# Two loads of first-layer weights begun later, one turn of R moved, and an earlier order put back, in a fused RWKV-7 and mixture kernel

## The chip, the cores and the metric

The kernel runs on one core of one Trainium2 chip. The metric is the device time of one execution in microseconds (us); the time before is the median of three runs. Profiles are of one execution each, with times counted from the start of its span.

## What is computed

The reference has two blocks. The first is an RWKV-7 recurrence over 768 tokens for 4 batches of 8 heads with 40 columns each. The second takes its output as 3072 rows of 320 columns and runs four two-layer experts (320 to 1024 to 320), mixed by given probabilities. All is in fp32.

```python
for t in range(S):                       # S = 768, state is D x D per head, D = 40
    y[:, :, t] = einsum('bhd,bhde->bhe', rt, state)
    Sa = einsum('bhde,bhe->bhd', state, at)
    state = state * wt[:, :, None, :] - einsum('bhd,bhe->bhde', Sa, bt)
    state = state + einsum('bhd,bhe->bhde', vt, kt)
...
p = domain_probs / (domain_probs.sum(-1, keepdims=True) + 1e-09)
for e in range(E):                       # E = 4
    h = np.maximum(x @ w1[e], 0.0)
    out += p[:, e:e + 1] * (h @ w2[e])
```

## The kernel before, in words

The recurrence is computed in chunks of 64 tokens. A *unit* is one chunk of two batches, so there are 24 units, numbered from 0. The work of a unit is split into generators, each advanced step by step with `run(generator, n)`, and the order of these calls is the order of TensorE's program:

- `within(q)` does what needs no state: it turns R and V (`turn_rv`), scans the decays (G), turns the tokens (NT, KT), and makes the scores (pc, pfe with pe, pev). In unit 1 its second step turns V and its third turns R: four transposes into `pRT` on TensorE and three copies into `RT` on ScalarE.
- `substitute(q)` solves a triangular system in blocks of 32: `M` is made by VectorE, and Z is built by VectorE in the first two units and by GpSimd in all later ones.
- `merge(q)` turns the solution (Qc, QTc) and makes two products, `pY` and `pQ`. Each is taken out of PSUM by four copies on ScalarE.
- `step(q)` joins unit and state: psat and pst, then `pxr`, then `pdy`, then xT, which the mixture takes as input.

The mixture runs on TensorE between these steps. w1 is loaded in *pieces* (half an expert: one DMA of 512 KB and two of 64 KB, `load_piece`); piece k serves the k-th product `ph`. A product has two parts: `up_last`, small matmuls for the last 64 input columns, and `up_main`, the large ones (8 and 8 in the program, 16 and 16 in the profile, which shows an fp32 matmul twice); the function `lead()` does `up_last` alone, ahead of its turn. w2 is loaded an expert at a time (`load_w2`, 1280 KB). From unit 2 on the second layer is done for two units at once by seven products (`p431`, `p75`, `p26`), whose PSUM tiles share three buffers with the two tiles of each `ph`. VectorE adds them to the output by `add`, and these additions are named out0, out1 and so on; out12 and out13 are the two that read the first `p75` of the first pair of units.

Three things set the order. TensorE goes in program order. VectorE's order is written by hand in `VECTOR_ORDER` (lines 20 to 30): each name is made to stand behind the one ahead of it. SyncE's queue gets the loads in the order of the calls, and each load takes one of eight DMA semaphores in turn, so that a load waits until the eighth load ahead of it has landed. The natural (not turned) B and K of a unit, `natB` and `natK`, have one buffer each: the loads for unit 2 wait until unit 1's n_tok and k_tok are made.

The start of unit 1 and the first pieces stand in the code so:

```python
load_piece()
load_piece()
run(m)
run(ws[1], 2)
go(load_raw(units[2], "A"))
load_w2(0)
load_piece()
load_piece()
run(ws[1], 1)
```

Here `m` is `merge(units[0])`, which has just made `pY`, and `ws[1]` is `within(units[1])`. Later comes `load(units[2], "BK")`, then `load_w2(1)`. In the loop over units, `EARLY` is 5; in iteration 5 a `lead()` stands between a step of `within` and the step of `step` that makes `pxr`.

Of the kernel before, what the change touches and what calls it, by code (L numbers as in the profile page):

```python
# [23 lines left out]
    YG3 SG3.0 S+3.1 gp5 SG3.1 1/gp5 RT5 N5 K5 sum_w4 out7 VC5.1 VC5.0 Qc4 QTc4 ET5.0 blocks5.0 blocks5.1 ET5.1 M5  # L24
    M05 Z15 Z25 RH4.0 RH4.1 G6.0 G6.1 gl6 G06 scan6 sum_a4 gll6 sum_w5 sum_w6 AT6 AG6 sum_a0 sum_a1 sum_a2 sum_a3
    SX4.0 SX4.1 sum_w7 VT6 sum_w8 Y4.1 Y4.0 S+4.0 YG4 SG4.0 S+4.1 gp6 SG4.1 1/gp6 RT6 N6 K6 out8 out9 out10 out11
    sum_a5 VC6.1 VC6.0 Qc5 QTc5 out12 out13 ET6.0 blocks6.0 blocks6.1 ET6.1 M6 M06 Z16 Z26 out14 out15 sum_w9 sum_a6
    G7.0 G7.1 gl7 G07 RH5.0 RH5.1 scan7 gll7 sum_a7 sum_a8 sum_a9 AT7 AG7 out16 out17 out18 out19 sum_w10 sum_w11
    SX5.0 SX5.1 sum_w12 sum_w13 sum_w14 sum_a10 sum_a11 out20 sum_a12 out21 sum_a13 VT7 out22 sum_a14 out23
"""  # L30
# [3 lines left out]
def kernel(  # L34
# [38 lines left out]
    nc = tc.nc  # L73
# [14 lines left out]
    names, made, stated_order = VECTOR_ORDER.split(), {}, []  # L88
# [273 lines left out]
    def load_w2(e):  # L362
        tc.keep_in_program_order(nc.sync.dma_start(out=w2_sb[e][:], in_=moe_w2[e].rearrange("(f p) d -> p f d", p=P)))
# [19 lines left out]
    def quarter(q):  # L383
        return slice(Q * q, Q * q + Q)

    def of_slot(x, s):

        return x.rearrange("p (j s) e -> p j s e", s=2)[:, :, s, :]
# [59 lines left out]
    def within(q):  # L448
# [19 lines left out]
        def turn_rv(which="VR"):  # L468
            VT = None
            if "V" in which:  # L470
                VT = sb.tile([P, 2 * NJ, L], FP32, name="VT", tag="turned", bufs=3)
            if "R" in which:
                q.RT = sb.tile([P, 2 * NJ, L], FP32, name="RT", tag="RT", bufs=2)
            for x, t in (("V", VT), ("R", getattr(q, "RT", None))):
                if x not in which:
                    continue
                if q.u >= PADDED:
                    noted(turn_raw(t[:], n["raw" + x][:]), x + "T", q.u)
                    continue
                p = turn(f"p{x}T", tok(n["padded" + x]), q.u == 1)[:].rearrange("p (j i t) -> p j i t", i=2, t=L)  # L480
                to = t[:].rearrange("p (i j) t -> p j i t", i=2)
                places = [(to[:, 0::2], p[:, 0::2])]
                places += [(to[half(r), 1::2], p[half(1 - r), 1::2]) for r in range(2)]
                for at, (o, p_) in enumerate(places):
                    if q.u == 2 and (x == "R" or at == 2):
                        noted(nc.vector.tensor_copy(out=o, in_=p_), x + "Tc", q.u, at)
                    else:
                        nc.scalar.copy(out=o, in_=p_)
            return VT

        if q.u == 1:
# [172 lines left out]
    def merge(q):  # L664


        Qc = sb.tile([P, H, Q], FP32, name="Qc", tag="q", bufs=2)
        QTc = sb.tile([P, H, Q], FP32, name="QTc", tag="q", bufs=2)
        keep(noted(nc.vector.transpose(out=dealt(Qc[:]), in_=q.Z), "Qc", q.u))
        ins = nc.vector.transpose(  # L670
            out=QTc[:].rearrange("p h r -> p (h r)"), in_=Qc[:].rearrange("p h c -> p (h c)"),
        )
        keep(noted(ins, "QTc", q.u))
        q.QT = QTs()
        for i in range(P // Q):
            ins = nc.gpsimd.tensor_copy(out=q.QT[quarter(i), :, quarter(i % 2)], in_=QTc[quarter(i)])  # L676
            tc.keep_in_program_order(ins)
        yield

        def two_heads(name, lhsT, rhs, to):  # L680
            p = big(name)
            for n in range(NJ):
                for r in range(2):
                    matmul(
                        out=p[half(r), n * 2 * Q:(n + 1) * 2 * Q], lhsT=lhsT[half(r), 2 * n:2 * n + 2, :],
                        rhs=rhs[half(r), 2 * n:2 * n + 2, :], start=True, stop=True,
                    )
            for r in range(2):
                for y in range(2):
                    src = p[quarter(2 * r + y), 0:H * Q].rearrange("p (n two t) -> p n two t", two=2, t=Q)[:, :, y, :]  # L690
                    with sooner(name == "pY"):
                        nc.scalar.copy(out=of_slot(to[quarter(2 * r)], y), in_=src)

        Y = Ys()
        two_heads("pY", q.below, QTc, Y)
        yield

        two_heads("pQ", Qc, Y, q.QT[:, :, quarter(1)])
        yield

# [357 lines left out]
    def run(gen, n=99):  # L1058
        if gen is None:
            return  # L1060
        for _ in range(n):
            if next(gen, gen) is gen:
                break
# [53 lines left out]
        load_padded(units[2], x)  # L1117
    load_piece()
    load_piece()
    run(m)  # L1120
    run(ws[1], 2)
    go(load_raw(units[2], "A"))
    load_w2(0)
    load_piece()
    load_piece()
    run(ws[1], 1)
    run(s, 3)
    run(ws[1], 1)
# [1 line left out]
    run(ws[1], 1)  # L1130
    run(s)
    load(units[2], "BK")
    load_w2(1)
    load_piece()
    run(ws[1], 2)
# [39 lines left out]
    for u in range(1, NU):  # L1175
        in_order[0] = True
        q = units[u]
        m = s_next = w = w_next = iter(())
        if u + 1 < NU:
            m, s_next = merge(units[u + 1]), begin_step(u + 1)  # L1180
            w_next = ws[u + 1]
        if u + 2 < NU:
            w = ws[u + 2]

        def gap(n, pieces=None):
            here[0] = at = 4 * u + n
            run(sum_ops, sums_at.get(at, 0))
            mix((1 if at in sparse else 2) if pieces is None else pieces)

        early = u < EARLY  # L1190
        if early:
            begin_later(len(later))
        ahead = u + 3 < NU and u in range(EARLY, EARLY + 3)
        if ahead:
            go(load_raw(begin(u + 3), "W"))
        if early:
            lead()
        if u == 1:
            run(s, 1)
            run(w_next)  # L1200
        else:
            run(w_next, 99 if early else 1)
            if u == EARLY:
                lead()
            run(s, 1)
        gap(0)


        if early:
            run(s, 1)  # L1210
        run(w, 1)
        if not early:
            run(w_next)
            run(s)

        if early:
            run(w, 1)
            gap(1, 2 if u + 1 == EARLY else None)
            run(s)
        if u == 1:  # L1220
            mixture_of_unit(q)
        elif q.bp:
            mixture_of_chunk(units[u - 1:u + 1], chunks_x[q.c])
        if not early:
            begin_later(len(later))
            run(w, 1)
            lead()
            todo[:2] = todo[1::-1]
            gap(1)
            run(m, 1)  # L1230

        if u + 3 < NU:
            if u == 1:
                go_now(load_raw(begin(4), "WVRA"))
            else:
                go(load_raw(units[u + 3] if ahead else begin(u + 3), "A" if ahead else "WA"))
            load(units[u + 3], "WBKV")
            if u > 1:
                later.extend(load_raw(units[u + 3], "VR"))
        run(w, 2)  # L1240

        soon = u in (2, 3, 4)
        if soon:
            run(w, 1)
        if early:
            run(m, 1)
        else:
            run(m, 1)
            run(s_next, 1)
            lead()  # L1250
            run(m, 1)
            if u + 3 < NU:
                ws.append(within(units[u + 3]))
                run(ws[u + 3], 1)
        if soon:
            substitute(units[u + 2], nc.gpsimd)
        gap(2)

        if u == 1:
            run(s_next, 1)  # L1260
            run(m, 1)
        if not soon:
            run(w, 1)
        if not soon and u + 2 < NU:
            with sooner(not early):
                substitute(units[u + 2], nc.gpsimd)
        if not early:
            lead()
            run(s_next, 1)
        if early:  # L1270
            run(w, 1)
        if early:
            ws.append(within(units[u + 3]))
            run(ws[u + 3], 1)
            if u > 1:
                run(m, 1)
                run(s_next, 1)
            run(m)
            if u == 3:
                begin_later(len(later))  # L1280
            gap(3, 1)
            run(s_next, 1)
        else:
            begin_later(len(later))
            gap(3)
        s = s_next
# [1 line left out]
    for piece in last:  # L1288
        piece()
    moved = [(out_, x) for out_, a_, u_ in ((45, 27, 9), (61, 37, 10)) for x in (f"sum_a{a_}", f"AT{u_}")]  # L1290
    for one, then in [*zip(names, names[1:]), *((f"out{n}", x) for n, x in moved), ("blocks0.3", "VCv1")]:
        tc.add_manual_dep(made[then].ins, made[one].ins.name, BEHIND, reason="stated order of VectorE")
    for k, then in ((13, "SX2.1"), (22, "SX5.0")):
        tc.add_manual_dep(made[f"piece{k}"].ins, made[then].ins.name, AFTER, reason="weights not beside dense products")
# [28 lines left out]
```

## Time and profile before

| What | Value |
|---|---|
| Median of three runs | 1083.35 us (1083.32 to 1083.89) |
| The profiled execution's own time | 1083.35 us |
| Its span in the profile | 1081.6 us, so 1.75 us lie around it |
| Mean granted TensorE clock | 0.996 |
| TensorE matmul busy | 1063.6 us (98%) |
| VectorE, GpSimd, ScalarE busy | 762.6, 492.7, 352.8 us |
| DMA | 122.19 MB, mean 113 GB/s |
| Chain that ended last | TensorE 92%, VectorE 3%, ScalarE 2%, DMA 1%, SyncE's queue 1%, issue 1% |

A span is read from its stages: the shares of the whole span hide the first 50 us, in which TensorE is not dense, and short stretches in which another engine is the one that never rests. "Issue" as the end of a wait means that the profile shows nothing that the engine waited for.

### The profile page before, as it was taken

The page shows a single profiled execution, that of the slowest core. Times are in us where ns is not written, and L with a number is a line of the kernel's source. Part 1 is how long each engine was busy: PE and PEld are TensorE (multiplying, and loading weights), DVE is VectorE, ACT ScalarE, POOL GpSimd, SP SyncE. Part 2 cuts the span into 40 slices and gives each one's busy share as a digit, 9 for nine tenths or more (in the row PEclk, how much of TensorE's full clock was granted, in tenths as well). Part 3 has the DMA queues.
Part 4 walks back from the last instruction along what each step waited for, and adds up shares of the span by engine and source line. Part 5 has one row for each costly group of instructions (what it writes and reads, how often), then busy time and mean ns, then how long its engine had stood idle before and what let it go on. Part 6 is the DMA issues. An engine that isn't in the chain of part 4 may idle for free.

```text
span 1081.6 us, 38611 instructions
## 1 busy us (share of the span) xinstructions
PE 1063.6 (98%) x16140; PEld 957.3 (89%) x16140; DVE 762.6 (71%) x1553; ACT 352.8 (33%) x954; POOL 492.7 (46%) x1274
## 2 busy tenths in 40 slices
PE   7899999999999999999999999999999999999998
PEld 7788888889999999999999999999999999998887
DVE  8777679897777866877777768668767776634343
ACT  3442434333333423324333334233233333221110
POOL 5216777755264373373562653733735626520000
PEclk9999999999999999999999999999999999999999
DMA  6877654445436445444354364454444532322320
GB/s 114 247 213 171 145 115 121 81 109 141 99 86 156 99 112 128 110 114 116 95 130 101 94 148 94 103 129 111 108 95 113 127 88 61 99 86 69 104 74 13
DMA packets 268869, 122.19 MB, mean 113 GB/s; under 512 B 213736, under 2 KB 242072, under 8 KB 268696
## 3 DMA queue, kind: packets, MB, share of 16 engines
q1 hardware_dynamic: 264872, 119.02, 45.5%
q8 instruction: 127, 2.08, 0.8%
q10 hardware_dynamic: 3824, 0.71, 0.4%
q14 instruction: 46, 0.38, 0.1%
HBM read 111.79 MB, written 3.93 MB: 107 GB/s over the span
## 4 chain that ended last, share of the span: by engine, by line
PE 92%; DVE 3%; ACT 2%; DMA 1%; SPq 1%; issue 1%; ACTq 0%; DVEq 0%
PE ph L110 39%; PE p L110 30%; PE po L110 3%; PE pdy L110 3%; PE pxr L110 2%; PE psat L110 2%; PE prn L110 2%; PE pfe L110 1%; PE pc L110 1%; PE pev L110 1%; PE pQ L110 1%; PE pe L110 1%; PE pNT L113 1%; PE pg L113 1%; PE pY L110 1%; PE pKT L113 1%
## 5 line engine op out<-in xcount | busy, mean ns | idle before, releaser
L110 PE MATMUL ph<-xT,w1p 128*128 128x256 f32 (+3 forms) x3040 | 441.3, 375 | 0.4 <-issue 0.4
L110 PEld LDWEIGHTS ph<-xT,w1p 64*64 64x64 f32 (+1 forms) x3040 | 336.5, 161 | 54.0 <-issue 13.8
L658 POOL TENSOR_TENSOR Z<-Z 128x31 f32<-128x31 f32 (+7 forms) x704 | 261.8, 372 | 55.2
L969 DVE TENSOR_TENSOR a<-hs 128x512 f32<-128x512 f32 x220 | 153.6, 716 | 106.2 <-ACT hs L846 106.2
L846 ACT ACTIVATE hs<-ph 128x512 f32<-128x512 f32 (+1 forms) x208 | 117.1, 564 | 321.5 <-PE ph L110 320.8
L645 POOL TENSOR_TENSOR Z<-M,Z 128x62 f32<-128x62 f32 (+7 forms) x352 | 144.4, 410 | 95.1 <-DVE M L631 69.2
L110 PE MATMUL p<-sums,a 128*128 128x160 f32 x1056 | 164.9, 299 | 0.0
L861 DVE SCALAR_TENSOR_TENSOR osb<-p,gate,osb 128x320 f32<-128x320 f32 (+1 forms) x243 | 107.9, 481 | 66.7 <-PE p L110 61.6
L110 PEld LDWEIGHTS p<-sums,a 128*128 128x128 f32 x1056 | 152.8, 190 | 2.2
L612 POOL COPY below<-F 32x256 f32<-32x256 f32 x48 | 21.3, 443 | 230.1 <-ACT F L567 228.5
L110 PEld LDWEIGHTS p<-w,hs 128*128 128x128 f32 x704 | 98.6, 190 | 8.9 <-issue 7.7
L110 PE MATMUL p<-w,hs 128*128 128x160 f32 x704 | 104.9, 302 | 0.3 <-DVE osb L861 0.3
L110 PE MATMUL p<-w,a 128*128 128x160 f32 x704 | 102.8, 299 | 0.0
L110 PEld LDWEIGHTS p<-w,a 128*128 128x128 f32 x704 | 98.0, 190 | 0.0
L676 POOL COPY QT<-QTc 32x256 f32<-32x256 f32 x96 | 40.4, 421 | 75.3 <-DVE QTc L670 67.1
L766 ACT COPY RS<-pxr 64x256 f32<-64x256 f32 x88 | 32.3, 367 | 104.4 <-DVE SX L446 51.6
L596 ACT COPY EV<-pev 64x160 f32<-64x160 f32 x96 | 23.0, 286 | 92.6 <-PE pev L110 92.3
L511 DVE RECIPROCAL gp<-gp 128x320 f32<-128x320 f32 x24 | 51.6, 2151 | 0.7
L615 DVE STREAM_TRANSPOSE M<-blocks 128x1024 f32<-128x1024 f32 x24 | 47.3, 1969 | 2.9 <-ACT blocks L608 2.9
L446 DVE COPY_PREDICATED VC<-mask_up,pc 128x256 f32<-128x256 int32 x48 | 18.7, 444 | 39.2 <-PE pc L110 39.2
L567 ACT COPY F<-pfe 128x256 f32<-128x256 f32 x48 | 15.6, 376 | 82.4 <-PE pfe L110 80.2
L110 PE MATMUL pdy<-VC,k_tok 64*64 64x104 f32 (+1 forms) x768 | 38.2, 259 | 0.0
(150 smaller groups left out, 1341.5 us busy)
## 6 DMA issues: line engine op xcount, KB each, us to landing
w1p<-in_moe_w_dram SPq DMA_DIRECT2D x95, 512.0 KB
w1p<-in_moe_w_dram SPq DMA_DIRECT2D x190, 64.0 KB
w<-in_moe_w_dram SPq DMA_DIRECT2D x4, 1280.0 KB
sums<-in_moe_w_dram SPq DMA_DIRECT2D x9, 512.0 KB
natW<-in_w_dram SPq DMA_DIRECT2D x48, 80.0 KB
natB<-in_b_dram SPq DMA_DIRECT2D x48, 80.0 KB
natK<-in_k_dram SPq DMA_DIRECT2D x48, 80.0 KB
out_dram<-osb SPq DMA_DIRECT2D x46, 80.0 KB
```

Source lines behind the costliest of these rows:

```text
L110: return stated(nc.tensor.matmul(**k))
L113: return stated(nc.tensor.transpose(**k))
L511: pin(noted(nc.vector.reciprocal(out=gp[:], in_=gp[:]), "1/gp", q.u))
L596: nc.scalar.copy(out=of_slot(q.EV[half(p)], i ^ p)[:, :, 0:D], in_=pev[i][half(p)])
L615: ins = nc.vector.transpose(out=M[:], in_=cols)
L645: ins = eng.tensor_tensor(out=Z[:, 1:3, 0:n, j + 1:Q], in0=M[:, j:j + 2, None, j + 1:Q].to_broadcast([P, 2, n, m]), in1=Z[:, here, 0:n, j: ...
L658: eng.tensor_tensor(out=z[:, 0], in0=z[:, 0], in1=z[:, x], op=ALU.add)
L676: ins = nc.gpsimd.tensor_copy(out=q.QT[quarter(i), :, quarter(i % 2)], in_=QTc[quarter(i)])
L766: nc.scalar.copy(out=RS[half(s), x ^ s::2], in_=prs[x][half(s)].rearrange("p (j i) t -> p j i t", i=2),)
L846: ins = nc.scalar.activation(out=h[:, i * HF // 2:(i + 1) * HF // 2, 0:n], in_=ph[i][:], func=ACTF.Relu,)
L861: ins = nc.vector.scalar_tensor_tensor(out=to, in0=p, scalar=sc, in1=to, op0=ALU.mult, op1=ALU.add)
L969: ins = nc.vector.tensor_tensor(out=t[:], in0=x, in1=y, op=op)
```

## The change

It has four edits. The third and fourth put an earlier order back.

1. **R of unit 1.** `merge(units[0])` is advanced by one step, then `within(units[1])`'s turn of R, and then the rest of each. On TensorE `pRT` now stands between `pY` and `pQ`, where it stood behind `pQ`. A stated order on ScalarE keeps the copies into `RT` behind the copies of `pQ`, as they were; for this the copies get names.
2. **Pieces 2 and 3.** The two `load_piece()` behind `load_w2(0)` move behind `load(units[2], "BK")`. On SyncE's queue natB and natK of unit 2 (four DMAs) now stand ahead of the six DMAs of these pieces.
3. **out12 and out13** move in VectorE's order from ahead of unit 6's masks and block copies (ET6.0, blocks6.0, blocks6.1, ET6.1) to behind them.
4. **The `lead()` of iteration 5** is taken away. On TensorE the small matmuls of piece 21's `up_last` go from ahead of `pxr` to behind it.

The instructions are the same in number and kind on every engine.

```diff
-    sum_a5 VC6.1 VC6.0 Qc5 QTc5 out12 out13 ET6.0 blocks6.0 blocks6.1 ET6.1 M6 M06 Z16 Z26 out14 out15 sum_w9 sum_a6
+    sum_a5 VC6.1 VC6.0 Qc5 QTc5 ET6.0 blocks6.0 blocks6.1 ET6.1 out12 out13 M6 M06 Z16 Z26 out14 out15 sum_w9 sum_a6
...
-                        nc.scalar.copy(out=o, in_=p_)
+                        noted(nc.scalar.copy(out=o, in_=p_), x + "Tc", q.u, at)
...
-                        nc.scalar.copy(out=of_slot(to[quarter(2 * r)], y), in_=src)
+                        ins = nc.scalar.copy(out=of_slot(to[quarter(2 * r)], y), in_=src)
+                    noted(ins, name + "c", q.u, 2 * r + y)
...
     load_piece()
     load_piece()
+    run(m, 1)
+    run(ws[1], 1)
     run(m)
-    run(ws[1], 2)
+    run(ws[1], 1)
     go(load_raw(units[2], "A"))
     load_w2(0)
-    load_piece()
-    load_piece()
     run(ws[1], 1)
...
     load(units[2], "BK")
+    load_piece()
+    load_piece()
     load_w2(1)
...
             run(w_next, 99 if early else 1)
-            if u == EARLY:
-                lead()
             run(s, 1)
...
-    for one, then in [*zip(names, names[1:]), *((f"out{n}", x) for n, x in moved), ("blocks0.3", "VCv1")]:
+    for one, then in [*zip(names, names[1:]), *((f"out{n}", x) for n, x in moved), ("blocks0.3", "VCv1"), ("pQc0.3", "RTc1.0")]:
```

## The prediction

> **What bounds the kernel now.** I read the page first, then the busy time by stage, then the chain of waits, then the timelines of SyncE, TensorE, VectorE and ScalarE where the change acts. The profiled execution took 1083.35 us, the median of the three runs; its span is 1081.6, and every sum below is made on 1083.35. "No change" means within 0.2% (2.17 us), about what a measurement of this kernel can tell.
>
> ```profile
> PE 1063.6 (98%) x16140; PEld 957.3 (89%) x16140; DVE 762.6 (71%) x1553; ACT 352.8 (33%) x954; POOL 492.7 (46%) x1274
> q8 instruction: 127, 2.08, 0.8%
> ```
>
> TensorE is the bound, so only its idle time can be won or added. The second line shows 127 DMA packets (2.08 MB, 16 KB each) on an instruction queue. TensorE has 2 x 16140 = 32280 instructions, and 32280 / 127 = 254: I read each packet as TensorE's next 254 or so instructions.
>
> ```profile
> 30.00:40.00 10.00, 8.11 (x188) 7.08 (x190) 8.33 (x16) 5.95 (x20) 3.75 (x6) 1.00 0.78 211
> 40.00:50.00 10.00, 7.62 (x190) 7.04 (x182) 4.11 (x11) 3.95 (x9) 1.82 (x3) 1.00 0.95 263
> 50.00:60.00 10.00, 9.74 (x106) 7.38 (x105) 9.44 (x32) 2.11 (x7) 0.00 (x0) 1.00 1.04 325
> 197.00:232.00 35.00, 34.51 (x520) 30.95 (x519) 34.27 (x65) 10.23 (x30) 26.84 (x56) 1.00 0.44 96
> ```
>
> By stage (columns: length, then busy time of TensorE, weight loads, VectorE, ScalarE, GpSimd; granted clock, DMA share, GB/s) the edits fall in two places. From 30 to 50 TensorE idles 1.89 + 2.38 us, and from 40 on the DMA engines are full. From 197 to 232 VectorE is busy 34.27 of 35.00, so it rests no more than TensorE does.
>
> ```profile
> 44.10 0.93 PE pfe L110 x62
> 45.03 2.38 issue
> 47.41 0.34 PE pfe L110 x2
> ```
>
> The chain of waits has its largest hole here: 62 of 64 matmuls run, then TensorE stands 2.38 us, and no semaphore ended the wait. The DMA view of 44.5 to 45.8 holds one instruction packet; in the packed trace it starts at 44.61 and takes 1.10. So I read the hole as TensorE out of instructions. By the count of TensorE's instructions (half a packet to a quarter packet before the packet's nominal place) I estimate that it was asked for at 39.7 to 40.4, and so waited over 4 us.
>
> ```profile
> 36.42 0.45 SPq L363 DMA_DIRECT2D w<-in_moe_w_dram  x1
> 36.92 4.16 SPq L343 DMA_DIRECT2D sums<-in_moe_w_dram  x6
> 41.17 3.53 SPq L240 DMA_DIRECT2D natB<-in_b_dram  x2
> ```
>
> SyncE's timeline names the traffic: w2 of expert 0 (1280 KB), then at once pieces 2 and 3 (six DMAs, 1280 KB). By the packet sizes in the trace, w2's 1280-byte packets move until about 42.3 on most DMA engines, piece 2 until about 44, then piece 3. The instruction packet came in the middle of piece 3, as if it stood in line behind all that had been begun before it.
>
> **The change part by part.**
>
> *Pieces 2 and 3 behind natB and natK.* The loads of natB wait for n_tok, which VectorE ends at 39.22 + 0.63 = 39.85. Four issues of about 0.63 follow, so piece 2 is begun at 42.5 in place of 36.92, and piece 3, whose first load takes the semaphore of w2, when w2 has landed: natB's second load waited for that until 44.08. When the instruction packet is asked for, only w2 and perhaps natB are ahead of it. Served after w2, it runs from 42.3 to 43.4; from its end to TensorE's restart it took 47.41 - 45.71 = 1.70, so TensorE could go on at 45.1 and the hole all but closes: gain 2.3. If all of natB and natK go first (4 x 512 packets of 160 bytes at 15 ns over 16 engines: 4 x 0.48 = 1.9), it is 47.0: gain 0.4. The ends are 2.38 and 0.4; I take 1.9, nearer to the first, since natB is begun at or after the asking. What the move could cost: piece 2 is first read at 58.43 and piece 3 at 61.0, over 10 us after they will land; natB and natK are read at 72.4. All hidden.
>
> The Trainium skill speaks against this twice. "Runtime: NRT & Kernel Launch", section "Instruction fetch mechanics", agrees on 16 KiB blocks of 256 instructions, but calls the crossing "mostly hidden"; by it the hole is not a fetch and this edit gains 0. "DMA: Bandwidth & Descriptors", section "Queues, rings and completion order", has each DMA engine alternate between queues packet by packet; by it an instruction packet would not wait out whole pieces. By either the sum ends at 1084.65. The row decides for me: no other cause of 2.38 us is in the trace.
>
> *R of unit 1 between pY and pQ.*
>
> ```profile
> 34.80 1.10 ACT L692 COPY QT<-pQ 32x128 f32<-32x128 f32 x4 [0.76 <-PE pQ L110]
> 35.92 1.13 ACT L488 COPY RT<-pRT 128x256 f32<-128x256 f32 x3
> 37.08 0.65 ACT L741 COPY SaT<-psat 128x256 f32<-128x256 f32 x2
> ```
>
> pRT (four transposes, 0.66) fills the hole between pY and pQ (32.86 to 33.53). But ScalarE's order is stated as before: QT, then RT, then SaT. It is without a pause from 34.80 to 37.7, and `pxr` waits for SaT, so TensorE only idles later, ahead of `pxr`. pg comes 0.4 earlier, but n_tok stays behind VectorE's masks of 38.55. Bounds: -0.4 (pRT's weight loads of 0.42 saved) to +0.4 (pRT not quite fitting and pushing pQ); taken 0.
>
> *out12, out13 and the lead of iteration 5.*
>
> ```profile
> 198.22 0.51 DVE L861 SCALAR_TENSOR_TENSOR osb<-p,gate,osb 128x320 f32<-128x320 f32 x1
> 198.76 0.39 DVE L861 SCALAR_TENSOR_TENSOR osb<-p,minus_gate,osb 128x160 f32<-128x160 f32 x1
> 199.58 4.75 PE L110 MATMUL ph<-xT,w1p 64*64 64x256 f32 x32
> 200.67 1.97 DVE L615 STREAM_TRANSPOSE M<-blocks 128x1024 f32<-128x1024 f32 x1
> 211.62 1.07 PE L110 MATMUL ph<-xT,w1p 64*64 64x256 f32 x16
> 211.90 1.20 ACT L746 COPY SX<-psat 64x160 f32<-64x160 f32 x4
> 212.51 0.92 PE L110 MATMUL pxr<-RT,SaT 64*64 64x64 f32 x31
> 233.17 0.67 DVE L283 STREAM_TRANSPOSE RT<-rawR 128x512 f32<-128x512 f32 x1
> 233.99 0.69 PE L110 MATMUL pc<-RT,VT 40*64 40x64 f32 x32 [0.84 <-DVE RT L283]
> ```
>
> The second tile of `ph` takes the PSUM buffer that these two additions empty. Now they end at 199.15, ahead of `ph` at 199.58. Behind the masks and block copies they end where M starts, about 200.7: TensorE waits 1.15. M itself does not move. Then the lead: its 16 matmuls fill 211.62 to 212.51 (0.89), while `pxr` could not go on before the second SX copy anyway (211.90 + 2 x 0.30 = 212.50). Behind `pxr` they hide nothing: +0.89, with 0.64 (their weight loads) and 1.07 (their row) as ends. Together 2.04.
>
> Part of it was lost anyway: TensorE stands 0.84 before `pc` at 233.99, waiting for VectorE's RT. VectorE becomes later only where it needs the late TensorE: its sums at 219.00 read the hs copy, whose product ends at 213.88 + 3.72 = 217.60; that copy takes 0.6, so there is a slack of 0.8, less 0.1 for release. So VectorE and with it `pc` move by 2.04 - 0.7 = 1.3. Ends: 0.6 (both terms a third smaller) and 2.04 (no slack used). I take 1.3.
>
> *What the head start meets.* TensorE comes 1.9 earlier, but w2 of expert 1 is begun only about 0.9 earlier (46.0 for 46.93), and the raw loads of unit 3 follow it. The nearest margin is A of unit 3, landed at 90.15 and read at 90.69: I give back 0.1, at most 0.5.
>
> Sum: -1.9 + 0 + 1.3 + 0.1 = -0.5, so **1082.8 us**.
>
> **The rivals.**
>
> 1. *Only the gain shows* (faster). The hole closes wholly (-2.38), and VectorE's full stretch hides both of the orders put back (0 to 0.2): 1081.0. For it: `pc` waits for VectorE, not TensorE. Against it: the hs copy ties VectorE to TensorE.
> 2. *The hole stays* (slower). At 45.03 the packet is again late, behind the 2048 small packets of natB and natK, or because traffic was never its cause. It decides if the packet starts after 44.2. Then nothing pays for the orders put back: +1.3 to +2.04, 1084.65 to 1085.4, and above 0.2% if the hole grows or opens again at a later packet.
> 3. *The clock falls.* The row of 20 to 30 has a granted clock of 0.66, half clock for 6.8 us, after idle stretches. With R moved, TensorE idles about 0.4 more before `pxr`. If that is enough, up to 3.4 is added: 1086. Against it: the 2.38 hole itself passed at 1.00.
> 4. *The edits of the start do nothing and the orders cost nothing*: 1083.35, inside no change.
>
> **How the numbers follow.** My forecast and the milder ends of the rivals lie within 0.2%: 1081.18 to 1085.52. Worked ends: 1083.35 - 2.38 + 0.6 = 1081.6 and 1083.35 - 0.4 + 2.04 = 1085.0. Chances: forecast 0.58, first rival 0.17, second 0.17, third 0.03, fourth 0.05. Of the first 0.14 lies beyond 0.2%; of the second and third 0.13. The range is 1081.0 to 1085.0.
>
> **What would show it.** Right: the issue hole before the last two pfe matmuls is under 1 us and the instruction packet there starts before 43.5; SaT keeps its distance from pQ's copies; a wait of about 1.1 at the second `ph` matmul near 199, released by VectorE; the wait before `pc` near 233 gone or changed little. Wrong: the hole as long as before, no new wait near 199, or a clock row under 1.00 after 30.

## The result, and the profile after

The changed kernel takes 1086.67 us (median of 22 runs, 1083.11 to 1090.21) against 1084.20 us (22 runs, 1082.75 to 1087.82) for the kernel before on the same chip: ratio 1.0022, 95% interval 1.0013 to 1.0031. It is about 2.4 us slower, outside the forecast range of 1081.0 to 1085.0.

The two profiled executions took 1088.11 and 1083.35 us, 1.4 above and 0.9 below these medians. So the traces say where time goes, and the timed runs say how much.

The hole at 45 is gone. The chain of waits of the kernel after:

```profile
44.10 1.00 PE pfe L110 x64
45.11 0.02 issue
```

In the packed trace the instruction packet now starts at 42.01 (44.61 before); 42.3 was forecast. But the head start does not last. SyncE's timeline (start, busy time, what was begun):

```profile
36.51 0.45 SPq L363 DMA_DIRECT2D w<-in_moe_w_dram  x1
40.68 1.31 SPq L240 DMA_DIRECT2D natB<-in_b_dram  x2
42.09 1.99 SPq L240 DMA_DIRECT2D natK<-in_k_dram  x2
44.12 3.60 SPq L343 DMA_DIRECT2D sums<-in_moe_w_dram  x6
47.76 0.59 SPq L363 DMA_DIRECT2D w<-in_moe_w_dram  x1
...
79.37 0.59 SPq L363 DMA_DIRECT2D w<-in_moe_w_dram  x1
80.06 5.21 SPq L343 DMA_DIRECT2D w1p<-in_moe_w_dram  x6
85.37 5.66 SPq L261 DMA_DIRECT2D rawA<-in_a_dram  x4
```

The six piece loads cost SyncE 4.16 us before, between 36.92 and 41.08, most of it inside its wait for n_tok (made at 39.85). Now they stand behind that wait and are 3.60 us of new work. At w2 of expert 1 this shows as 0.83 us only (begun at 47.76, 46.93 before), since natB and natK no longer wait 3.1 us for earlier loads to land. Then the lateness grows: w2 of expert 2 is begun at 58.82 (57.28), w2 of expert 3 at 79.37 (76.34), and A of unit 3 at 85.37 (81.71); that A lands at 93.33 (90.15). The chain of waits shows what A's third load waited for, the landing of a piece:

```profile
80.06 10.15 DMA w1p<-in_moe_w_dram
90.20 0.02 issue
90.22 0.31 SPq L261
90.53 0.04 issue
90.58 2.75 DMA rawA<-in_a_dram
```

The DMA engines moved less while the pieces were not yet begun. The rows from 42 to 48 of the kernel after, of the one before, and of two experiments told below, e7 and e10 (the last column is GB/s):

```profile
42.00:48.00 6.00, 6.00 (x158) 5.42 (x157) 3.54 (x9) 3.48 (x9) 0.84 (x2) 1.00 0.72 172
42.00:48.00 6.00, 3.62 (x125) 3.32 (x124) 1.52 (x6) 1.86 (x5) 0.00 (x0) 1.00 0.97 264
42.00:48.00 6.00, 6.00 (x153) 5.58 (x155) 3.54 (x10) 3.47 (x9) 0.84 (x2) 1.00 0.75 185
42.00:48.00 6.00, 6.00 (x150) 5.58 (x151) 3.54 (x10) 3.46 (x9) 3.29 (x7) 1.00 0.99 266
```

What the late A does stands in VectorE's timeline, then TensorE's (start, busy time, and in brackets the idle time ahead and what ended it):

```profile
93.45 0.71 DVE L283 STREAM_TRANSPOSE AT<-rawA 128x512 f32<-128x512 f32 x1 [5.06 <-DMA rawA<-in_a_dram]
```

```profile
95.83 1.60 PE L110 MATMUL pxT<-Y,sums 128*128 128x128 f32 x12 [0.72 <-DVE Y L782]
100.00 0.86 PE L113 MATMUL pNT<-ident,n_tok 128*128 128x128 f32 x4 [2.57 <-DVE n_tok L532]
```

By stage (the columns of the rows before; first the kernel after, then before):

```profile
90.00:100.00 10.00, 6.71 (x40) 4.77 (x34) 6.45 (x12) 0.48 (x1) 8.29 (x22) 1.00 0.68 132
100.00:110.00 10.00, 10.00 (x213) 8.80 (x215) 3.21 (x9) 3.34 (x8) 3.78 (x13) 0.83 0.65 149
197.00:232.00 35.00, 33.79 (x570) 29.93 (x563) 31.20 (x58) 11.22 (x34) 26.68 (x57) 1.00 0.50 113
```

```profile
90.00:100.00 10.00, 10.00 (x136) 8.31 (x138) 8.22 (x15) 1.90 (x5) 8.35 (x22) 1.00 0.76 175
```

TensorE loses 3.29 us in two waits, and behind them its granted clock is 0.83 from 100 to 110 (0.57 from 100 to 104): the clock record in the packed trace has half clock from 100.32 to 103.73, which by itself is 1.7 us. The orders put back show where they were forecast. `ph` goes on at 203.61, 0.10 behind the end of VectorE's second addition (203.13 and 0.38; TensorE's row calls the wait "issue"), and the 0.84 ahead of `pc` is gone:

```profile
203.13 0.38 DVE L862 SCALAR_TENSOR_TENSOR osb<-p,minus_gate,osb 128x160 f32<-128x160 f32 x1
203.61 2.58 PE L110 MATMUL ph<-xT,w1p 64*64 64x256 f32 x20 [0.62 <-issue]
216.58 0.69 PE L110 MATMUL pxr<-RT,SaT 64*64 64x64 f32 x30 [0.43 <-ACT SX L747]
237.47 0.69 PE L110 MATMUL pc<-RT,VT 40*64 40x64 f32 x32
```

To add this up I use TensorE's *lag*: the start of a matmul in one trace minus the start of the same matmul in the trace before, as a median over a stretch (minus is ahead). Stretches in the time of the kernel before:

| Kernel | 36–42 | 60–70 | 102–106 | 130–140 | 180–190 | 214–220 | 250–260 |
|---|---|---|---|---|---|---|---|
| after | 0.00 | −2.37 | +2.95 | +2.89 | +2.88 | +4.64 | +3.55 |
| e1: pieces alone | +0.39 | −1.97 | +1.10 | +4.36 | +4.11 | +3.75 | +3.44 |
| e2: R alone | −0.02 | +1.50 | +1.50 | +1.48 | +1.47 | +1.10 | +1.32 |
| e3: orders alone | +0.38 | +0.12 | +0.12 | +0.12 | +0.17 | +1.92 | +0.92 |
| e7: pieces between B and K | +0.43 | −1.93 | +4.44 | +4.38 | +4.36 | +6.12 | +5.08 |
| e8: idle time filled | −0.15 | −2.50 | +0.73 | +0.94 | +1.57 | +2.58 | +2.09 |
| e9: pieces 9, 10 behind A | +0.23 | −2.13 | −1.92 | +4.58 | +4.38 | +4.87 | +3.66 |
| e10: pieces from GpSimd | +0.50 | −1.85 | −1.06 | −0.25 | −0.36 | +1.05 | +0.03 |
| e11: e10, orders kept | +0.02 | −2.33 | −0.92 | −0.91 | −0.90 | −1.13 | −0.83 |
| e12: e11, stream reordered | +0.16 | −1.12 | −1.12 | −0.50 | −0.65 | −1.02 | −0.14 |

So after gains 2.37 at the hole, loses 5.3 near 95 to 104, 1.8 near 199 and 212, and gets 1.1 back near 233. From 260 to the end its trace loses another 1.2 with no wait of TensorE behind it; the other traces lose between 0 and 1.3 there, whatever their edit, so I put this down to the executions; no run shows its cause.

### The profile page after: what moved, and what is told of

Same layout as the page of the kernel before. It is cut to its first block, busy times and chain, and to the rows that moved or that the text cites. A ratio compares the mean times of both kernels' runs of the same rounds, so it can differ in the third digit from the quotient of the medians.

```text
span 1086.4 us, 38608 instructions
## 1 busy us (share of the span) xinstructions
PE 1066.6 (98%) x16140; PEld 958.7 (88%) x16140; DVE 763.0 (70%) x1553; ACT 352.8 (32%) x954; POOL 493.1 (45%) x1274
## 4 chain that ended last, share of the span: by engine, by line
PE 90%; DVE 4%; DMA 3%; ACT 1%; SPq 1%; issue 1%; ACTq 0%; DVEq 0%
PE ph L110 39%; PE p L110 31%; PE pdy L110 3%; PE pxr L110 2%; PE psat L110 2%; PE prn L110 2%; PE po L110 2%; DMA w1p<-in_moe_w_dram 2%; PE pfe L110 1%; PE pc L110 1%; PE pQ L110 1%; PE pev L110 1%; PE pe L110 1%; PE pNT L113 1%; PE pY L110 1%; PE pKT L113 1%
## 5 line engine op out<-in xcount | busy, mean ns | idle before, releaser
L658 POOL TENSOR_TENSOR Z<-Z 128x31 f32<-128x31 f32 (+7 forms) x704 | 258.2, 367 | 55.2
L645 POOL TENSOR_TENSOR Z<-M,Z 128x62 f32<-128x62 f32 (+7 forms) x352 | 148.5, 422 | 95.1 <-DVE M L631 69.3
```

The costliest lines, as they stand in the source:

```text
L645: ins = eng.tensor_tensor(out=Z[:, 1:3, 0:n, j + 1:Q], in0=M[:, j:j + 2, None, j + 1:Q].to_broadcast([P, 2, n, m]), in1=Z[:, here, 0:n, j: ...
L658: eng.tensor_tensor(out=z[:, 0], in0=z[:, 0], in1=z[:, x], op=ALU.add)
```

## The experiments

The ratios are to the kernel before, run beside them. The edits on the orders, on R and on the pieces are those of the change; each diff shows the rest.

**e1: the pieces alone.** The second edit on the kernel before.

> The kernel before with the second edit alone: pieces 2 and 3 begun behind natB and natK of unit 2. Theory (the lost time is a late A of unit 3, because six piece loads of about 0.6 us each are now issued, and 1280 KB moved, after SyncE's wait for n_tok instead of during it): the hole of 2.38 us at 45 is gone, rawA of unit 3 lands near 93.3 in place of 90.15, VectorE waits about 5 us for it, TensorE loses about 5.3 us between 85 and 102 and is about 2.9 us behind the kernel before from there to the end, with no new wait at 199 or 216: about 2.5 to 3 us slower. Rival one (the A is late through the R turn or through the orders, not through the pieces): the hole is gone, rawA lands before 91, and the time is 2 us below the kernel before. Rival two (the hole is not tied to the pieces): hole unchanged, time unchanged.

Ratio 1.0012 (0.9999 to 1.0024), 1086.19 against 1084.36 us. The hole is gone, and A of unit 3 lands at 93.07. VectorE reads it at 93.19. In TensorE's timeline one wait follows at unit 3, and one at unit 4, whose A is late as well:

```profile
99.57 0.66 PE L113 MATMUL pNT<-ident,n_tok 128*128 128x128 f32 x4 [2.62 <-DVE n_tok L532]
122.20 3.13 PE L110 MATMUL ph<-xT,sums 64*64 64x128 f32 x22 [1.88 <-ACT hs L846]
```

Both rivals fall: in the trace this edit alone closes the hole, makes A late, and loses 3.1 us at unit 3 (at full clock) and 3.3 more at unit 4. The timed runs say less, 1.3 us by the ratio in place of the expected 2.5 to 3, and not quite clear of none. The ratios of e1, e2 and e3 add up to that of the whole change (1.0012, 1.0006 and 1.0004 for 1.0022).

**e2: R alone.** The first edit on the kernel before.

> The kernel before with the first edit alone: unit 1's R turned between unit 0's pY and pQ. Theory: the hole of 2.4 us at 45 stays, rawA of unit 3 lands near 90.2, TensorE's place at 111 moves by less than 0.4 us: within 0.1% of the kernel before. Rival one (this edit delays the loads): rawA later by over 1 us and the time up by 2 us or more.

Ratio 1.0006 (0.9994 to 1.0018). A lands at 90.25, so R does not delay the loads. In this execution the hole was longer, 2.99 us, and a lower clock followed it (TensorE's timeline, then the row by stage):

```profile
47.99 0.33 PE L110 MATMUL pfe<-AT,KT 64*64 64x64 f32 x2 [2.99 <-issue]
```

```profile
48.00:52.00 4.00, 4.00 (x42) 3.60 (x46) 2.95 (x5) 1.79 (x5) 0.84 (x2) 0.70 0.80 232
```

That lies behind the +1.5 of the table, where under 0.4 was expected. Whether the longer hole belongs to R or to that execution stays open; a cost of R of its own is below what these runs can tell.

**e3: the orders alone.** The third and fourth edit on the kernel before.

> The kernel before with the third and fourth edit alone: out12 and out13 behind the masks and block copies of unit 6, and no lead in iteration 5. Theory: up to 195 us nothing changes; TensorE waits 0.6 to 1.2 us at the second ph matmul near 199 and 0.4 to 0.9 us ahead of pxr near 212; the waits of 0.30 at 225 and 0.81 at 233 go; net 0.6 us slower (0.3 to 1.3), near what the timing can tell. Rival (what is lost in VectorE stays lost, and the wait at 233 stays): 1.9 to 2.0 us slower.

Ratio 1.0004 (0.9992 to 1.0015). In the trace the lag grows by 1.2 at 199 and by 0.6 at 212; the waits at 225 and 233 go and give back 1.1. Net 0.75, as after's 0.67, near the milder end of the prediction (0.6).

**e4: A of unit 3 earlier.** The changed kernel with

```diff
-    go_now(load_raw(units[3], "W"))
+    go_now(load_raw(units[3], "WA"))
...
-    go_now(load_raw(units[3], "A"))
```

> The changed kernel, with the four loads of A of unit 3 issued directly behind those of its W, ahead of pieces 7 to 10 and of w2 of expert 3. Theory (TensorE's loss of 5.3 us is VectorE's wait for this A): rawA lands before 82, the wait of 5 us is gone; next late is natW of unit 3, which lands near 93 and holds gp until then, about 1.1 us later than VectorE could begin; so TensorE gets back about 3.6 us by 111 (4.7 at most, if natW lands by 92) and keeps it to the end: 3 to 4 us faster than the changed kernel, 1 us faster than the kernel before. Rival (A is late, but something else that is as late holds the same path, so its cover is all that goes): under 1 us faster than the changed kernel.

Ratio 1.0035 (1.0022 to 1.0047). The remedy was wrong: there is one raw A tile. Issued there, the loads stand ahead of unit 2's turn of it, so unit 2 reads A of unit 3 and waits for it (no other loads of A stand between this turn and unit 3's at 94.37):

```profile
79.33 0.71 DVE L283 STREAM_TRANSPOSE AT<-rawA 128x512 f32<-128x512 f32 x1 [8.13 <-DMA rawA<-in_a_dram]
```

It tells nothing of unit 3. It only moves the wait to 75.84, where TensorE stands 5.07 us.

**e5 and e6: w2 of expert 3 behind unit 3's loads.**

```diff
-                if q.u == 0 and e + 2 < E:
-                    load_w2(e + 2)
+                if q.u == 0 and e == 0:
+                    load_w2(2)
...
     load(units[3], "WBKV")
+    load_w2(3)
```

> The changed kernel, with w2 of expert 3 (1280 KB, first read near 112) begun behind unit 3's A and its W, B, K and V by token, in place of ahead of pieces 9 and 10. Theory (TensorE's 5.3 us between 85 and 104 come from unit 3's A, which lands at 93.3 behind weights that nobody needs yet: 3.3 us of waits and, by the clock row, some 2 us of half clock behind them): A lands near 88, VectorE waits under 0.7 us for it, natW lands before 92, no wait over 0.5 us at pNT, the granted clock from 100 to 104 is 1.00; TensorE is 2.2 us ahead of the kernel before at 111 and 1.5 to 2 us ahead at 260: about 5 us faster than the changed kernel, 0.2% faster than the kernel before. Rival (SyncE's issues and not the transfers ahead set when A lands): A lands after 91 and the gain is under 2 us. Rival two (w2 of expert 3 is then too late itself): a wait at expert 3's down product near 107.

> The kernel before with the first and second edit and with w2 of expert 3 begun behind unit 3's loads, so without the third and fourth edit. Theory: as the run above up to 195; from there no wait at 199 and at 212, but the waits of 0.30 and 0.81 near 225 and 233 return: 0.6 us faster than the run above, 2.2 to 2.4 us faster than the kernel before (0.2%). Rival (VectorE's stretch from 197 to 235 gives the orders back): as the run above within 0.2 us in the trace.

Ratios 1.0076 (1.0063 to 1.0089) and 1.0071 (1.0058 to 1.0084). My second rival, with my own error behind it: I had taken a later unit's product for expert 3's first. TensorE reads this w2 at 90.6. The waits of e5 from 88 to 104:

```profile
PE po L110 <- DMA w<-in_moe_w_dram: 11.1, 1, 11.1
```

So w2 of expert 3, begun 3 us late in the changed kernel, has only 2.0 us to spare there (landed 88.54, read 90.53), and cannot make room for A. Pieces 9 and 10 can, with 15 and 25 us.

**e7: pieces between natB and natK.**

```diff
-    load(units[2], "BK")
+    load(units[2], "B")
     load_piece()
     load_piece()
+    load(units[2], "K")
```

> The changed kernel with pieces 2 and 3 between natB and natK of unit 2 in place of behind both: they are begun at about 42.0 in place of 44.1, and w2 of expert 1 at the same time as in the changed kernel. Theory one (the stream is late because the DMA engines move little from 42.5 to 47.5): they move 2 us more, A of unit 3 lands 1.5 to 2 us earlier, near 91.5, the wait at pNT falls under 1 us, no half clock: 3 to 4 us faster than the changed kernel. Theory two (it is late by the six issues on SyncE, which stand in line in either order): A lands within 0.5 us of 93.3, under 1 us faster. In both the hole at 45 stays closed.

Ratio 1.0021 (1.0009 to 1.0034), as the changed kernel. SyncE's timeline:

```profile
42.45 4.49 SPq L343 DMA_DIRECT2D sums<-in_moe_w_dram  x6
47.05 2.12 SPq L240 DMA_DIRECT2D natK<-in_k_dram  x2
49.21 0.62 SPq L363 DMA_DIRECT2D w<-in_moe_w_dram  x1
```

The pieces are begun 1.7 earlier, but natK now waits behind them, and w2 of expert 1 is begun 1.45 later than in the changed kernel. A lands at 94.78, 1.45 later too, in place of earlier. Neither theory's forecast came. Theory one is not refuted by this, since its condition was not met: from 42 to 48 the DMA engines moved 185 GB/s, hardly more than in the changed kernel (172). What the run shows is that w2 of expert 1 and A are late by the same 1.45.

**e8: the idle time filled.** In the changed kernel, for unit 3's pNT alone:

```diff
-    def turn(name, src, pinned=False):
+    def turn(name, src, pinned=False, warmth=0):
 
         p = big(name)
+        for _ in range(warmth):
+            tc.keep_in_program_order(matmul(out=p[:, 0:P], lhsT=ident[:], rhs=ident[:], start=True, stop=True))
...
-            nc.scalar.copy(out=t[:].rearrange("p j t -> p (j t)"), in_=turn("p" + name, tok(x), q.u == 1)[:])
+            nc.scalar.copy(out=t[:].rearrange("p j t -> p (j t)"), in_=turn("p" + name, tok(x), q.u == 1, 8 if q.u == 3 and name == "NT" else 0)[:])
```

> The changed kernel with eight matmuls of the identity (about 0.2 us each) ahead of unit 3's pNT, into the tile that pNT then overwrites: they fill most of the 2.57 us in which TensorE waits for n_tok. Theory (half of the loss is the clock, which falls behind the idle time): the granted clock from 100 to 104 is 1.00 in place of 0.57, and TensorE's lag behind the kernel before at 111 is about 1 us in place of 2.9, with the wait for n_tok as before. Rival (the loss is the wait alone, and the clock row has another cause): the row stays under 0.7 and the lag at 2.9. The order further on may differ, so that the stretch is to be read and not the total time.

Ratio 1.0013 (1.0003 to 1.0022). TensorE's timeline and the window behind it:

```profile
96.41 1.95 PE L110 MATMUL pNT<-ident 128*128 128x128 f32 x16
99.20 0.66 PE L113 MATMUL pNT<-ident,n_tok 128*128 128x128 f32 x4 [0.84 <-DVE n_tok L534]
```

```profile
100.00:104.00 4.00, 4.00 (x85) 3.37 (x83) 1.94 (x5) 2.19 (x5) 2.15 (x9) 1.00 0.87 225
```

n_tok is nearly as late as in the changed kernel (pNT begins at 99.20 for 100.00, A landed 0.6 earlier), yet the clock stays at 1.00, and the loss between 60 and 104 is 3.2 in place of 5.3. So 1.7 of the 5.3, by after's clock record, were the clock; the difference of the two executions is 2.1, and the earlier A is part of it. e1 passed a wait of 2.62 at full clock with nothing filled in, so that the filling kept the clock is argued from where the idle time lay (last section).

**e9: pieces 9 and 10 behind unit 3's loads.** The changed kernel with

```diff
-                used(at + 2 * e + 2)
+                if q.u or e != 2:
+                    used(at + 2 * e + 2)
...
     load(units[3], "WBKV")
+    used(6)
```

> The changed kernel, with pieces 9 and 10 of w1 (first read at 105 and 117) begun behind unit 3's A and its W, B, K and V by token; w2 of expert 3 stays ahead of them, since the run with it behind showed that TensorE reads it at 90.6 and not near 112. Theory (A is late because it stands in SyncE's stream behind weights that aren't needed yet): A is begun near 80 and lands right behind w2 of expert 3, at 88.7 to 89.5 in place of 93.3; VectorE waits about 1 us for it, TensorE at most 0.7 at pNT, granted clock 1.00 from 100 to 104; TensorE 1.5 to 2.4 us ahead of the kernel before at 111 and about 1 to 1.8 at 260: 4 to 5 us faster than the changed kernel. Rival (pieces 9 and 10 then come too late themselves): a wait ahead of ph near 101 or 112. Rival two (A is held by the landing of the transfers that had its semaphores before it): A after 91, gain under 2.5 us.

Ratio 1.0026 (1.0015 to 1.0037). At unit 3 the theory holds: A lands at 89.73, VectorE waits 1.17, TensorE not at all, and it is still 1.92 ahead at 104. But then A of unit 4 stands behind pieces 9 to 12. VectorE waits 5.59 for it at 118.71, and in TensorE's timeline and windows:

```profile
121.75 1.63 PE L110 MATMUL ph<-xT,sums 64*64 64x128 f32 x15 [3.82 <-ACT hs L847]
```

```profile
120.00:124.00 4.00, 2.25 (x19) 1.93 (x20) 3.18 (x6) 1.91 (x6) 3.53 (x7) 0.50 0.80 125
```

6.5 us are lost 20 us later, and in place of 4 to 5 us faster the kernel is as slow as the changed one. One late load mended, the next in the stream was late.

**e10: the six loads from GpSimd.** The changed kernel with

```diff
-    def load_piece():
+    def load_piece(eng=nc.sync):
...
-            ins = nc.sync.dma_start(out=to, in_=src)
+            ins = eng.dma_start(out=to, in_=src)
...
     load(units[2], "BK")
-    load_piece()
-    load_piece()
+    load_piece(nc.gpsimd)
+    load_piece(nc.gpsimd)
```

> The changed kernel with the six loads of pieces 2 and 3 begun by GpSimd, behind its AT of unit 1 (which ends at 40.3), in place of by SyncE behind natK of unit 2; bytes, places in memory and the order of TensorE, VectorE and ScalarE stay. Theory (A of unit 3 is late by the six issues, 3.6 us, that SyncE does behind its wait for n_tok): w2 of expert 1 is begun near 44.2 in place of 47.8, the whole stream of SyncE is 2 to 3.6 us earlier, A lands at 89.5 to 91, VectorE's wait for it is under 2.5 us, no half clock from 100 to 104, TensorE 1 to 2.4 us ahead of the kernel before at 111: 3.5 to 5 us faster than the changed kernel. Theory two (A is late by the bytes that did not move from 42.5 to 47.5): the pieces' first packets move near 42.5 and again the stream is earlier, by up to 5 us. Rival (the instruction packet, asked for near 40, meets the pieces again): the hole at 45 returns with 1 to 2.4 us. Rival two (GpSimd takes over 0.9 us for each issue): its copy of below at 45.9 is late, and with it unit 1's masks and scores.

1084.66 against 1084.82 us, ratio 1.0000 (0.9990 to 1.0010): by the ratios 2.4 us faster than the changed kernel (3.5 to 5 were expected), with the same bytes and the same order on TensorE, VectorE and ScalarE. GpSimd's timeline, then SyncE's:

```profile
40.74 3.71 POOL L343 DMA_DIRECT2D sums<-in_moe_w_dram  x6
```

```profile
45.23 1.23 SPq L363 DMA_DIRECT2D w<-in_moe_w_dram  x1
```

A of unit 3 lands at 90.70, 2.6 earlier than in the changed kernel, and w2 of expert 1 is begun 2.5 earlier. From 42 to 48 the DMA engines move as much as before the change (266 and 264 GB/s), so both theories had their condition met. VectorE still waits 1.85 for this A, since it is itself earlier, and 2.46 for unit 4's. GpSimd took 0.62 us for an issue, about as long as SyncE (3.60 / 6).

**e11 and e12: versions to beat both.** e11 is e10 without the third and fourth edit. e12 is e11 with e9's move, and pieces 11 and 12 behind unit 4's raw loads:

```diff
-                if q.u or e != 2:
+                if q.u or e < 2:
...
                 go_now(load_raw(begin(4), "WVRA"))
+                used(8)
```

> The kernel before with the first and second edit, the six loads of pieces 2 and 3 begun by GpSimd as in the run before, and without the third and fourth edit. Theory: as that run up to 195 (TensorE about 0.3 us ahead of the kernel before, since A of unit 4 takes back part of the closed hole); from there the waits of the orders put back are missing (1.2 at 199 and 0.6 at 212), those at 225 and 233 return: 0 to 0.4 us ahead at 260, 0.4 to 0.7 us faster than the run before, and the same as the kernel before within what can be measured. Rival (VectorE's full stretch gives the orders back): the same place at 260 as the run before, within 0.1 us.

> The run above, with SyncE's stream put more nearly in the order in which things are read: pieces 9 and 10 behind unit 3's A and its loads by token, and pieces 11 and 12 (first read near 119 and 132) behind unit 4's W, V, R and A. Theory (what eats the closed hole is only the lateness of the small loads of units 3 and 4 behind weights): A of unit 3 lands at 86 to 88.5, A of unit 4 is read without a wait of over 0.5 us, no wait over 0.5 us at pNT near 97 or at ph near 118, granted clock 1.00 throughout; TensorE 1.8 to 2.4 us ahead of the kernel before at 130 and at 260: 0.15 to 0.2% faster than it. Rival (the stream as a whole is too slow, so that what is put behind is late in turn): a wait of 1 us or more at ph near 101, 114 or 119 for piece 9, 10 or 11, or at gp of unit 4 for its W.

1083.30 and 1083.07 against 1084.64 us, ratios 0.9986 (0.9978 to 0.9995) and 0.9985 (0.9976 to 0.9993): both are faster than the kernel before, by 1.3 and 1.6 us, and so than the changed one; between the two these runs show no difference. e11 keeps 0.9 of the 2.33 us that the hole gave, more than the 0 to 0.4 expected. In e12 VectorE waits for no A at all (it reads unit 3's at 89.58 without an idle time ahead, where e11 waits 2.33), and TensorE gives back 0.6 up to 130, where e11 gives back 1.4. But in this execution the hole was back by half, so it had less to keep:

```profile
46.27 0.33 PE L110 MATMUL pfe<-AT,KT 64*64 64x64 f32 x2 [1.08 <-issue]
```

Its instruction packet started at 43.69, those of e10 and e11 at 42.50 and 42.16. The forecast 1.8 to 2.4 ahead was not reached: 1.12 at 104 and 0.14 at 260, with a wait of 2.15 us at 226 for an addition on VectorE, which is busy without a pause from 222.4 to 229.2; what made it late was not traced.

## Why the prediction was wrong, step by step

- **The hole.** Right in cause and size. It was tied to the pieces (e1), and closing it gave 2.37 for a forecast of 1.9, with the packet at 42.01 for 42.3. In the four traces with a hole (before, e2, e3, e12) TensorE went on 1.5 to 1.7 us after the packet's end.
- **R.** Right on TensorE and ScalarE: lag 0.00 at 36 to 42 in after, and the copies into SaT at the same 37.08 as before. But the prediction took n_tok at its 0.63 of before, and it took 1.43. In all fourteen traces it takes 1.42 to 1.44 where GpSimd's AT of unit 1 begins ahead of it, and 0.63 to 0.66 where that begins behind; ten of the eleven kernels with R's edit are of the first kind, the three without it of the second.
- **The orders put back.** Right in mechanism and place. Gross 1.8 for 2.04; the slack that swallows part of it was 1.1 for 0.7; net 0.7 for 1.3, within the ends.
- **"What the head start meets".** This step failed: "I give back 0.1, at most 0.5". It was 5.3 in the trace: 3.29 of waits of TensorE, and 1.7 of half clock behind them. Three things were wrong in it:
  1. *SyncE's time.* I had w2 of expert 1 begun at 46.0, from four issues of 0.63 behind n_tok and six more. natB was begun at 40.68 and not 39.85, behind the longer n_tok, and natK took 1.99. So the pieces began at 44.12 and not 42.5, and w2 at 47.76. Before, the six issues had mostly filled a wait; moved behind it, they were work. And I took the stream behind w2 to keep its distance, but 0.83 of lateness there became 3.18 at A's landing. In the list of what the move could cost, I looked at the pieces and at natB and natK ("All hidden", which held), and not at what is queued behind them on SyncE.
  2. *The margin.* I had named the right load: A of unit 3, 0.54 us from being late. But a TensorE that is 2.4 us earlier wants it 2.4 us earlier (VectorE was free at 88.39). Even on time for the kernel before, it would have been 1.8 late. With 3.2 of lateness in the stream VectorE's wait was 5.06.
  3. *The clock.* The third rival named half clock behind idle time, and put it ahead of `pxr` at 37. It came at 100, behind 2.57 us of idle, and cost 1.7 by the clock record. So the sign named for being wrong, a clock row under 1.00 after 30, did come.
- **The rivals.** None had a transfer of a later unit that turns late: that was the case missing on the slow side. The sum with the measured terms is −2.4 + 5.3 + 0.7 = +3.6 (+3.55 in the table at 260); the timed runs say +2.4. The two profiled executions are 4.8 apart, and 2.3 of that is their distance from the medians.
- **Not settled.** That moving the pieces makes the loads late is shown (e1), and that beginning them from GpSimd brings back 2.6 of the 3.2 us (e10). But e10 moves both SyncE's issues and the bytes to an earlier time, and no run moves one without the other, so how much each counts stays open. The begin of w2 of expert 1 alone does not set it: e10 begins it 1.7 earlier than the kernel before, and its A lands 0.55 later. How much of the growth from 0.83 to 3.18 is the wait of each load for the landing of the eighth ahead of it was not taken apart.

## What to carry to other kernels

Loads that are issued while their queue would have waited anyway can be nearly free; here, put behind the wait, they made a load 40 us later land 3.2 us late. When an edit makes the bound engine earlier, ask of each later load whether it lands earlier too, and price a margin as margin less head start. Before reordering a stream, list each transfer's landing and first reader: mending one late load here made the next one late (e9), and among these runs VectorE waited for neither only where the issues were also taken off the queue (e12).

## What the runs showed of the hardware

- **The clock fell behind short idle times, and where these lay decided.** The clock records of all fourteen traces change only at multiples of 3.41 us from one another. Laid on this grid, from 40 us on the clock fell to half behind the stretches of 3.41 us in which TensorE was idle for 1.82 (e2), 1.88 (e1), 1.94 (e9), 2.20 (e4), 2.57 (after), 2.72 (e7) and 3.41 us (e5, e6), and held behind every other one up to the end of the work, with 1.82 (e6) and 1.81 (e12) idle as the most. So the waits of 2.38 (before), 2.11 (e3) and 2.62 us (e1, at 97) passed at 1.00: each lay across a border, with 1.55, 1.67 and 1.38 on its longer side. Without the filling e8 would have had about 2.2 in one stretch. In the first 30 us the clock fell behind less, 1.44 (before), so this is no fixed bound. The Trainium skill, "TensorE: Matmul & The Clock Gate", section "What's actually happening", has a free-running window of 3413 ns that watches how busy TensorE is, and calls the result run-variable; that agrees with the grid, and with 1.88 falling and 2.62 not. Its rule in "HAM oscillation — how this bites in real kernels", no idle gap over about 3.4 us, does not: 1.88 was enough.
- **An instruction packet came later where bulk loads of another queue had been begun ahead of it.** With the two pieces begun by SyncE near 37 it started at 44.61 to 45.24 and the hole was 2.11 to 2.99 us (before, e2, e3). With them behind natB or natK it started at 41.81 to 42.73, and the hole was gone. With the pieces on GpSimd's queue, begun at 40.27 to 40.74, it started at 42.16 to 43.69; the hole was closed twice and 1.08 once.
